# Paired 64-row mask products, filler work for TensorE, an early GpSimd drain, a last tile in halves and loads on release, in an attention-and-experts kernel

## The chip, the cores and the metric

The kernel runs on one core of one Trainium2 chip. The metric is the device time of one execution in microseconds (us). Each run comes with a state: **slow** runs (over 1.5% above the fastest of the same kernel on that chip) are left out of the comparisons of times here, and only times taken in the same call, on the same chip, are compared with each other. Traces are also read across chips, and three traces are of slow runs; the text says where. That turned out to matter: six calls on at least five chips appear below (the first call's chip is not on record), and the mean of the fast runs of the kernel before is 217 to 229 us, depending on the chip. In the five calls of the experiments these means rest on only 2 or 3 of its 7 to 11 runs, so ratios to the kernel before are uncertain by some 0.01 to 0.03; differences between variants of one call rest on 2 to 6 runs each.

A **hole** below is idle time of TensorE between two products. "issue" in a line means that the engine waited for nothing that the profile shows, and the granted clock is the share of full speed that the profile records for TensorE.

## The reference, cut to what matters

```python
# q, k, v: (4, 8, 768, 64).  Attention in a window of +-15 tokens, plus 24 block summaries
k_sum = k.reshape(B, H, 24, 32, D).max(axis=3);  v_sum = v.reshape(B, H, 24, 32, D).mean(axis=3)
scores = concat(where(abs(i - j) < 16, q k^T / 8, -1e9), q k_sum^T / 8 + log(32))
x = softmax(scores) @ concat(v, v_sum)          # -> (3072 tokens, 512)
# top-1 mixture of 8 experts, with a bias on the gate that depends on the token's modality
logits = x @ w_gate + modality_bias[modality_id];  e = argmax(logits)
out[t] = softmax(logits)[t, e] * relu(x[t] @ w1[e]) @ w2[e]      # w1: 512x1024, w2: 1024x512
```

With this draw all 3072 tokens go to two experts, 1564 to expert 3 and 1508 to expert 5. In tiles of 256 tokens that makes eleven full tiles, one of 228 and one of 28, and the one that comes last, the thirteenth, is that of 28.

## The kernel before

Sixteen **pairs** (a batch and two heads) go through the attention one after the other. For each, TensorE transposes k, v and q, forms scores in two halves, ScalarE takes the exponential into `pT`, and TensorE multiplies it with the values. From pair 10 on, expert work is put between the attention's steps in **units**, quarter tiles of the first layer or halves of the second. GpSimd issues the input and weight loads, scatters the finished rows into a sorted buffer `xs` with indirect DMAs, and stores each expert tile's result (`ot`) to `out` with indirect DMAs.

The parts that the change touches (cut):

```python
NMASK = 10
NV, NK = 8, 3                                   # input buffers: eight pairs deep
...
# keys(): two zero columns beside the transposed keys, one 128-wide product per tensor
nc.tensor.matmul(pb.bitcast(FP32)[:, 0:C8 * P8 // 2 + 2:C8 * P8 // 2 + 1],
                 ident[0:P8], identp[0:P8, 0:2], skip_group_check=True)
...
# scores(): the mask is added on TensorE for pairs 0 to 9, multiplied in on VectorE after that
if n < NMASK:
    for h in range(2):
        nc.tensor.matmul(pss[h], ident, bterm[:, 6 * half:6 * half + 6, :],
                         start=True, stop=False, skip_group_check=True)
for tl in range(6):
    for h in range(2):
        nc.tensor.matmul(pss[h][:, tl, :], kv[rr, 0, t, :], qT[...], start=n >= NMASK, stop=True, ...)
nc.scalar.activation(pT..., two, AF.Exp, scale=SCALE)
if n >= NMASK:
    nc.vector.tensor_tensor(pT[0:WK], pT[0:WK], bmask[...], op=ALU.mult)
...
UNITS = {10: "000111", 11: "111011", 12: "111011", 13: "111011", 14: "111011", 15: "101110"}
ENLIST = {9: 0, 11: 1, 15: 2}                   # after which pair a batch's tiles are listed
WAT = {2: "w0", 4: "w1", 6: "w2", 7: "w3", 8: "w4", 9: "w5", 10: "w6 w7"}   # weights in halves
def issue(n, i):
    if i < 3:
        if n + 4 < np_:
            load(n + 4, (i,))                   # inputs four pairs ahead
...
# the end: the thirteenth tile runs whole, all 256 rows
with ExitStack() as ifs:
    for j in range(NSURE, FIN):
        ifs.enter_context(tc.If(nt > j))
        ...
        drain(pending.popleft())
```

The softmax here doesn't subtract the row's maximum and nothing guards it: scores larger than these inputs give would overflow.

Of the kernel before, what the change touches and what calls it, by code (L numbers as in the profile page):

```python
# [18 lines left out]
TAKE = [2, 4, 2]  # L19
# [4 lines left out]
def kernel(  # L24
# [48 lines left out]
    NMASK = 10  # L73
    NV, NK = 8, 3
# [6 lines left out]
    def load(n, which=(0, 1, 2)):  # L81
        b, cc = pairs[n]
        for i in which:
            name, src = (("kn", k), ("vn", v), ("qn", q))[i]
            dst = work.tile([P8, 2, C8, D], FP16, tag=name, bufs=NV, name=name)
            nc.gpsimd.dma_start(
                dst.rearrange("p h c d -> p h (c d)"),
                src[b, 2 * cc:2 * cc + 2].rearrange("h (p c) d -> p h (c d)", c=C8),
            )
            loaded.setdefault(n, []).append(dst)  # L90
# [10 lines left out]
    identp = const.tile([128, 130], FP16, name="identp")  # L101
    ident = identp[:, 2:130]
    nc.vector.memset(identp[:, 0:2], 0.0)
    nc.vector.tensor_scalar(ident, cidx, pidx, None, op0=ALU.is_equal)

    def borders(i):
        kv, vb = kvs[i], vbs[i]
        nc.vector.memset(kv[:, :, :, KR:128], 0.0)
        nc.vector.memset(vb[0:WK, :, :, D:D + 1], 1.0)
        nc.vector.memset(vb[WK:KR, :, :, D:D + 1], 32.0)  # L110

    borders(0)
# [7 lines left out]
    band = const.tile([128, 2, 64], FP32, name="band")  # L120
    nc.vector.tensor_scalar(band[:, 0, :], cidx[:, 0:64], pidx, 0.0, op0=ALU.subtract, op1=ALU.is_lt)
    nc.vector.tensor_scalar(band[:, 1, :], cidx[:, 0:64], pidx, -32.0, op0=ALU.subtract, op1=ALU.is_gt)
    bmask = const.tile([128, NT, 64], FP16, name="bmask")
    nc.vector.tensor_tensor(bmask, band[:, 0:1, :].to_broadcast([128, NT, 64]),
                            band[:, 1:2, :].to_broadcast([128, NT, 64]), op=ALU.mult)
    edge = const.tile([128, 2], FP32, name="edge")
    nc.vector.tensor_scalar(edge[:, 0:1], pidx, 16.0, None, op0=ALU.is_ge)
    nc.vector.tensor_scalar(edge[:, 1:2], pidx, 80.0, None, op0=ALU.is_lt)
    nc.vector.tensor_scalar_mul(bmask[:, 0, :], bmask[:, 0, :], edge[:, 0:1])
    nc.vector.tensor_scalar_mul(bmask[:, NT - 1, :], bmask[:, NT - 1, :], edge[:, 1:2])  # L130
# [8 lines left out]

    bterm = const.tile([128, NT, 64], FP16, name="bterm")  # L140
    nc.vector.tensor_scalar(bterm, bmask, -1.0, 30000.0, op0=ALU.add, op1=ALU.mult)
    nc.vector.memset(bterm[WK:128], 0.0)

# [76 lines left out]
    def load_weights(u, e, which=(0, 1), part=None, **kw):  # L220
        for i in which:
            src, dst = ((moe_w1, w1b[u]), (moe_w2, w2b[u]))[i]
            src = src[ds(e, 1)].rearrange("a (c p) f -> p (a c) f", p=128)
            if part is not None:
                n = dst.shape[1] // 2
                src, dst = src[:, ts(part, n)], dst[:, ts(part, n)]
            nc.gpsimd.dma_start(dst, src, **kw)  # L227
# [4 lines left out]
    def keys(n):  # L232

        kv, vs = kvs[n % NK], None
        for i in range(2):
            src = loaded[n][i]
            pb = bank([128, 1024], FP16, "pk")
            for c in range(C8):
                for h in range(2):
                    nc.tensor.transpose(pb[64 * h:64 * h + 64, 2 + P8 * c:2 + P8 * c + P8], src[:, h, c, :],  # L240
                                        ident[0:P8, 0:P8])

            nc.tensor.matmul(pb.bitcast(FP32)[:, 0:C8 * P8 // 2 + 2:C8 * P8 // 2 + 1],  # L243
                             ident[0:P8], identp[0:P8, 0:2], skip_group_check=True)
            if i and n < NSUM:
                vs = pb[:, C8 * P8 + 4:C8 * P8 + 4 + 2 * NB].bitcast(FP32)
                for c in range(C8):
                    for h in range(2):
                        nc.tensor.matmul(vs[64 * h:64 * h + 64, :], src[:, h, c, :], ind[0:P8],
                                         start=(c == 0), stop=(c == C8 - 1), skip_group_check=True)  # L250
            nc.scalar.copy(  # L251
                kv[:, i, :, 0:WK].rearrange("p t (s c) -> p t s c", c=C8),
                bass.AP(pb.tensor, pb.offset, [pb.ap[0], [8, NT], [1, 12], [P8, C8]]))
        st[n] = dict(kv=kv, vb=vbs[n % NK], vs=vs)

    def summaries(n):
        kv = st[n]["kv"]
        ks = work.tile([128, 2, NT, 2], FP16, tag="ks", name="ks")
        nc.vector.reduce_max(ks[:, 0], kv[:, 0, :, 16:80].rearrange("p t (g s) -> p t g s", g=2), axis=AX.X)  # L259
        vs = st[n]["vs"]  # L260
        if vs is not None:
            nc.vector.tensor_copy(ks[:, 1].rearrange("p t g -> p (t g)"), vs)
        with nc.allow_low_precision(reason="summed in fp32, kept as v is"):
            vs is not None or nc.vector.reduce_sum(ks[:, 1], kv[:, 1, :, 16:80].rearrange("p t (g s) -> p t g s", g=2), axis=AX.X)  # L264
        nc.gpsimd.tensor_copy(kv[:, :, :, WK:KR],  # L265
                              ks.rearrange("p a t g -> p a (t g)")[:, :, None, :].to_broadcast([128, 2, NT, NB]))
# [11 lines left out]
    def blocks(n):  # L278

        kv, vb = st[n]["kv"], st[n]["vb"]  # L280
        for half in range(2):
            pv = bank([128, 6, 128], FP16, "pv")
            for tl in range(6):
                nc.tensor.transpose(pv[:, tl, :], kv[:, 1, 6 * half + tl, :], ident)  # L284
            (nc.vector.tensor_copy if half or n < NMASK and n % 4 else nc.scalar.copy)(  # L285
                vb[0:KR, 6 * half:6 * half + 6, :, 0:D],
                pv[0:KR].rearrange("p t (h d) -> p t h d", h=2))

    def scores(n, half):
# [4 lines left out]
        if n < NMASK:  # L294
            for h in range(2):
                nc.tensor.matmul(pss[h], ident, bterm[:, 6 * half:6 * half + 6, :],
                                 start=True, stop=False, skip_group_check=True)
        for tl in range(6):
            t = 6 * half + tl
            for h in range(2):  # L300
# [3 lines left out]
                                 start=n >= NMASK, stop=True, skip_group_check=True)  # L304
        pT = work.tile([128, 2, 6, 64], FP16, tag="pT", bufs=3, name="pT")
        nc.scalar.activation(pT.rearrange("p h t s -> p h (t s)"), two, AF.Exp, scale=SCALE)  # L306
        if n >= NMASK:
            nc.vector.tensor_tensor(
                pT[0:WK], pT[0:WK],
                bmask[0:WK, None, 6 * half:6 * half + 6, :].to_broadcast([WK, 2, 6, 64]), op=ALU.mult)  # L310
# [219 lines left out]
    def turn(i):  # L530
# [8 lines left out]
        (nc.scalar.copy if ended[0] >= sum(TAKE) - 4 else nc.vector.tensor_copy)(xg, px.rearrange("p c a s -> p c (a s)"))  # L539
# [38 lines left out]



    UNITS = {10: "000111", 11: "111011", 12: "111011", 13: "111011", 14: "111011", 15: "101110"}
    ENLIST = {9: 0, 11: 1, 15: 2}
# [64 lines left out]
    WAT = {2: "w0", 4: "w1", 6: "w2", 7: "w3", 8: "w4", 9: "w5", 10: "w6 w7"}  # L647

    def issue(n, i):
        if i < 3:  # L650
            if n + 4 < np_:
                load(n + 4, (i,))
            return
        for what in WAT.get(n, "").split():
            p = int(what[1:])
            if p % 4 == 0:
                gv[p // 4] = nc.gpsimd.value_load(guess[0:1, p // 4:p // 4 + 1], min_val=0, max_val=E - 1)
            load_weights(p // 4, gv[p // 4], which=(p // 2 % 2,), part=p % 2)
            if p == 3:
                guessed[0] = 1  # L660
            if p == 7:
                guessed[0] = NTILE + NWB
                ahead()
# [4 lines left out]
    load(3)  # L668
    borders(1)
    queries(0)  # L670
    side.append(early_constants())
    side.append(later_constants())
    for n in range(np_):
# [5 lines left out]
        issue(n, 0)  # L679
# [3 lines left out]
        issue(n, 1)  # L683
        tick(1 if n < 10 else 2)
        scatter()
        pump(u[1])
        if n == 0:
            keys(1)
            summaries(1)
            borders(2)  # L690
        if n + 1 < np_:
            queries(n + 1)
        if n:
            values(n - 1, 1)
# [5 lines left out]
        issue(n, 2)  # L700
        tick(1 if n < 10 else 2)
        scatter()
        pump(u[3])
        if n + 2 < np_:
            keys(n + 2)
        tick(1 if n < 10 else 2)
        pump(u[4])
        values(n, 0)
        issue(n, 3)
# [3 lines left out]
        if n + 2 < np_:  # L713
            summaries(n + 2)
        tick(1 if n < 10 else 2)
# [27 lines left out]
    while todo or len(pending) > 1:  # L743
        if ended[0] == i0 + NSURE - 2:
            nt = nc.values_load(r["li"][0:1, NSURE + 1, 0:1], min_val=NSURE, max_val=FIN)
        while unit():
            pass
    with ExitStack() as ifs:  # L748
        for j in range(NSURE, FIN):
            ifs.enter_context(tc.If(nt > j))  # L750
            if j == NSURE + 1:
                drain(take("more", r["cf"], FIN - NSURE - 1, i0 + j, KM))
            if j > NSURE:
                rows(lists["more"], j - NSURE - 1, i0 + j)
                weights(lists["more"], j - NSURE - 1, i0 + j)
                pending.append(expert_tile(i0 + j))
            drain(pending.popleft())
# [28 lines left out]
```

## Time and profile before

| | us |
|---|---|
| median of 3 runs | 229.16 (228.28 to 229.37) |
| span of the profiled execution | 226.3 |
| pair 1's to pair 10's first exponential | 53.80 |
| pair 10's first exponential to pair 11's | 14.15 |
| pairs 11 to 14 | 45.15 |
| end of the last store to the end | 9.4 |

The stages are cut at the start of a pair's first exponential. The view of busy times by stretch gives them; the columns are the stretch, its length, the busy time of TensorE's products, its weight loads, VectorE, ScalarE and GpSimd (instruction counts in brackets), the granted clock, the DMA engines' share and GB/s. For the kernel before:

```profile
19.14:72.94 53.80, 47.96 (x1257) 37.63 (x1252) 40.23 (x127) 41.27 (x51) 33.55 (x48) 0.92 1.00 161
72.94:87.09 14.15, 9.96 (x155) 8.14 (x154) 7.64 (x28) 6.45 (x9) 5.84 (x10) 0.58 0.96 181
87.09:132.24 45.15, 41.97 (x647) 29.18 (x645) 29.02 (x83) 29.63 (x45) 20.08 (x30) 0.97 0.53 126
```

In the first stretch TensorE works for 48 of 54 us and the DMA engines are full (share 1.00); in pair 10 the clock has fallen to 0.58.

### The profile page before, as it was taken

The numbers are of one execution on the slowest core, as the hardware profiler recorded it, in microseconds if no ns is written. First come the engines' busy times: TensorE is split into PE (matmuls) and PEld (weight loads), VectorE is DVE, ScalarE is ACT, GpSimd is POOL, SyncE is SP. The second block draws the span as 40 slices with busy tenths as digits, with TensorE's granted clock in tenths as the row PEclk, the third lists the DMA queues.
The fourth block names the chain that finished last, engine by engine and source line by source line (L and its number), as shares of the span: only waits on it lengthen the run. The fifth ranks groups of instructions, "written<-read, shape, count | busy, mean of one in ns | idle before, by whom it ended". The sixth has DMA issues, their size and how long they took to land. (4 is left out here: it accounts for less than half of the span.)

```text
span 226.3 us, 7116 instructions
## 1 busy us (share of the span) xinstructions
PE 189.3 (84%) x2948; PEld 136.1 (60%) x2948; DVE 104.5 (46%) x338; ACT 133.7 (59%) x180; POOL 111.3 (49%) x166
## 2 busy tenths in 40 slices
PE   0699998799895569999999599899976999999900
PEld 0487786587775458585767366675652766776500
DVE  6349975666994728784667182639200000000000
ACT  2589899458886428686675254455532667656410
POOL 8556545446895336680406507047673355462220
PEclk9999999859997559999999979999998899999975
DMA  4999999939999978998201303422333123321100
GB/s 74 178 185 151 130 185 171 190 53 147 225 163 206 226 159 133 206 157 256 104 3 72 122 1 118 125 89 80 122 106 138 51 91 120 112 82 54 53 19 0
DMA packets 20092, 27.47 MB, mean 121 GB/s; under 512 B 2876, under 2 KB 16468, under 8 KB 20052
## 3 DMA queue, kind: packets, MB, share of 16 engines
q0 software_dynamic: 17424, 24.40, 53.5%
q1 hardware_dynamic: 2628, 2.54, 3.9%
q8 instruction: 25, 0.41, 0.8%
q14 instruction: 15, 0.12, 0.2%
HBM read 85.46 MB, written 10.44 MB: 424 GB/s over the span
## 5 line engine op out<-in xcount | busy, mean ns | idle before, releaser
L556 PE MATMUL ph<-xg,w1b 128*128 128x256 f16 x416 | 51.7, 277 | 3.5 <-issue 1.7
L568 PE MATMUL pmo<-w2b,hT 128*128 128x512 f16 x208 | 49.8, 386 | 2.7 <-ACT hT L558 2.5
L556 PEld LDWEIGHTS <-w1b 128*128 128x128 f16 x416 | 39.7, 99 | 11.3 <-issue 3.0
L558 ACT ACTIVATE hT<-ph 128x512 f16<-128x512 f32 x52 | 31.0, 598 | 26.2 <-PE ph L556 18.4
L574 POOL DMA_INDIRECT out_dram<-ot,at x26 | 26.2, 1007 | 37.4 <-ACT ot L572 33.2
L251 ACT COPY kv<-pk 128x1152 f16<-128x1152 f16 x32 | 34.8, 1125 | 13.7 <-PE pk L243 10.7
L568 PEld LDWEIGHTS <-hT 128*128 128x128 f16 x208 | 19.5, 99 | 24.3 <-ACT hT L558 3.8
L572 ACT ACTIVATE ot<-pmo,xr 128x512 f32<-128x512 f32 x26 | 17.9, 690 | 24.7 <-PE pmo L568 16.5
L365 POOL DMA_INDIRECT xs<-xb,posi x24 | 25.8, 1074 | 13.1 <-issue 6.8
L306 ACT ACTIVATE pT<-pss 128x768 f16<-128x768 f32 x32 | 26.1, 816 | 7.2 <-PE pss L302 7.2
L265 POOL COPY kv<-ks 128x576 f16<-128x576 f16 x16 | 10.9, 683 | 39.2 <-DVE ks L264 15.8
L542 DVE SCALAR_TENSOR_TENSOR at<-gm,xr 128x2 uint32<-128x2 f32 x13 | 2.3, 182 | 40.9 <-DMA xr<-xs,gi 36.9
L332 DVE TENSOR_TENSOR xb<-po,rec 128x384 f16<-128x384 f32 x32 | 17.8, 556 | 1.0
L325 DVE RECIPROCAL rec<-po 128x6 f32<-128x6 f32 x32 | 6.1, 190 | 25.8 <-PE po L322 18.2
L275 ACT COPY qT<-pq 128x768 f16<-128x768 f16 x16 | 12.9, 809 | 7.8 <-PE pq L273 5.1
L259 DVE TENSOR_REDUCE ks<-kv 128x24 f16<-128x768 f16 x16 | 15.1, 944 | 3.0 <-ACT kv L251 3.0
L302 PEld LDWEIGHTS <-kv 64*128 64x128 f16 x384 | 8.3, 99 | 12.8 <-issue 11.8
L322 PE MATMUL po<-vb,pT 120*64 120x65 f16 x384 | 13.2, 203 | 3.2 <-issue 3.0
L284 PE MATMUL pv<-identp,kv 128*128 128x128 f16 x192 | 15.4, 236 | 0.0
L302 PE MATMUL pss<-qT,kv 64*128 64x64 f16 x384 | 12.5, 199 | 2.4 <-issue 2.2
L285 DVE COPY vb<-pv 120x768 f16<-120x768 f16 x23 | 12.2, 552 | 4.7 <-PE pv L284 4.5
L240 PE MATMUL pk<-identp,kn 96*64 96x96 f16 x256 | 9.3, 220 | 5.2 <-DMA kn<-in_k_dram 5.2
(130 smaller groups left out, 273.2 us busy)
## 6 DMA issues: line engine op xcount, KB each, us to landing
w1b<-in_moe_w_dram POOLq DMA_DIRECT2D x13, 1024.0 KB
w2b<-in_moe_w_dram POOLq DMA_DIRECT2D x13, 1024.0 KB
kn<-in_k_dram POOLq DMA_DIRECT2D x16, 192.0 KB
vn<-in_v_dram POOLq DMA_DIRECT2D x16, 192.0 KB
qn<-in_q_dram POOLq DMA_DIRECT2D x16, 192.0 KB
xr<-xs SPq DMA_DIRECT2D x8, 272.0 KB, 3.9
w1b<-in_moe_w_dram POOLq DMA_DIRECT2D x4, 512.0 KB
w2b<-in_moe_w_dram POOLq DMA_DIRECT2D x4, 512.0 KB
```

The lines of the kernel that those rows point to most:

```text
L251: nc.scalar.copy(kv[:, i, :, 0:WK].rearrange("p t (s c) -> p t s c", c=C8), bass.AP(pb.tensor, pb.offset, [pb.ap[0], [8, NT], [1, 12], [P8 ...
L259: nc.vector.reduce_max(ks[:, 0], kv[:, 0, :, 16:80].rearrange("p t (g s) -> p t g s", g=2), axis=AX.X)
L284: nc.tensor.transpose(pv[:, tl, :], kv[:, 1, 6 * half + tl, :], ident)
L302: nc.tensor.matmul(pss[h][:, tl, :], kv[rr, 0, t, :], qT[rr, ts(t, 8), :].rearrange("p s c -> p (s c)"), start=n >= NMASK, stop=True, skip ...
L306: nc.scalar.activation(pT.rearrange("p h t s -> p h (t s)"), two, AF.Exp, scale=SCALE)
L332: nc.vector.tensor_tensor(xo, po[:, :, :, 0:D], rec.unsqueeze(3).to_broadcast([128, 2, 3, D]), op=ALU.mult)
L365: apart("xs", nc.gpsimd.indirect_dma_start(out=xs[:, :], out_offset=bass.IndirectOffsetOnAxis(ap=posi[:, j:j + 1], axis=0), in_=xb[:, c, : ...
L556: nc.tensor.matmul(ph[:, f, :], w1[:, c, ts(2 * f2 + f, 128)], xg[:, c, :], start=(c == 0), stop=(c == NCD - 1))
L558: nc.scalar.activation(hT[:, 2 * f2:2 * f2 + 2, :], ph, AF.Relu)
L568: nc.tensor.matmul(po, hT[:, f, ts(s2, 128)], w2[:, f, :], start=(f == 0), stop=(f == NF - 1))
L572: nc.scalar.activation(ot, po, AF.Copy, scale=gt)
L574: apart("out", nc.gpsimd.indirect_dma_start(out=out[:, :], out_offset=bass.IndirectOffsetOnAxis(ap=at[:, s2:s2 + 1], axis=0), in_=ot[:], i ...
```

## The change

Its intent is to take work and waits off TensorE: two 64-row mask products side by side (the traces show starts 3 ns apart, and 173 ns apart for the two before) in place of one 128-row product each; filler products before the data arrive, so that the clock is full when they do (its records begin, with full speed, at 5.34 us instead of 13.17); expert work a pair later, so that it doesn't wait for its rows; loads issued when a buffer is released, weights in quarters; the thirteenth tile in halves of 128 tokens, the second skipped if empty; and GpSimd's DMA queue drained some tiles before the end. Smaller parts aren't shown: in pairs 10 to 15 VectorE takes over most of ScalarE's copies of v, ScalarE copies the first expert tile's rows, and GpSimd clears a strip of the keys and values in each pair. The core of it (cut):

```diff
-    NMASK = 10
-    NV, NK = 8, 3
+    NV, NK = 3, 3
...
+    busy(9)                       # 9 products of 512 columns on zeros, 3 more within pair 0's keys
...
-            nc.tensor.matmul(pb.bitcast(FP32)[:, 0:C8 * P8 // 2 + 2:C8 * P8 // 2 + 1],
-                             ident[0:P8], identp[0:P8, 0:2], skip_group_check=True)
+            for h in range(2):
+                nc.tensor.matmul(pb[64 * h:64 * h + 64].bitcast(FP32)[:, 0:C8 * P8 // 2 + 2:C8 * P8 // 2 + 1],
+                                 src[:, h, C8 - 1, :], warm[0:P8, 0:2], skip_group_check=True)
...
-        if n < NMASK:
-            for h in range(2):
-                nc.tensor.matmul(pss[h], ident, bterm[:, 6 * half:6 * half + 6, :], ...)
+        for h in range(2):
+            rr = slice(64 * h, 64 * h + 64)
+            nc.tensor.matmul(pss[h], bterm[rr, :], ident[rr, None, rr].to_broadcast([64, 6, 64]), ...)
...
-        if n >= NMASK:
-            nc.vector.tensor_tensor(pT[0:WK], pT[0:WK], bmask[...], op=ALU.mult)
...
-    UNITS = {10: "000111", 11: "111011", 12: "111011", 13: "111011", 14: "111011", 15: "101110"}
-    ENLIST = {9: 0, 11: 1, 15: 2}
+    UNITS = {11: "111111", 12: "111111", 13: "111111", 14: "111111", 15: "101110"}
+    ENLIST = {9: 0, 12: 1, 15: 2}
...
-    WAT = {2: "w0", 4: "w1", 6: "w2", 7: "w3", 8: "w4", 9: "w5", 10: "w6 w7"}
+    WAT = {1: 1, 2: 1, 3: 1, 4: 2, 5: 1, 6: 2, 7: 2, 8: 2, 9: 2, 10: 2}      # quarters
+    def more(n, which):           # called where a buffer's last reader has been issued
+        if n + NV < np_:
+            load(n + NV, which)
...
-        scatter()
+        early = n - 1 not in ENLIST
+        scatter(early)            # and a second scatter(early) later in the pair
...
         if ended[0] == last - 2:
             nt = nc.values_load(...)
+            more_than = left(r, NSURE)
+            nc.gpsimd.drain()
...
-            drain(pending.popleft())
+            expert_half(i, 0)
+            with tc.If(more_than > 128):
+                expert_half(i, 1)
```

## The prediction

> **What bounds the kernel now.** I read the sliced page first (where is TensorE not full, where is its clock low), then the TensorE timeline around every hole, then the pair periods, and last the end. The page's slices (5.66 us each):
>
> ```profile
> PE   0699998799895569999999599899976999999900
> ACT  2589899458886428686675254455532667656410
> PEclk9999999859997559999999979999998899999975
> DMA  4999999939999978998201303422333123321100
> ```
>
> TensorE is full nearly everywhere, so it is the bound, except in the first slice, around slices 12 to 14, at slice 22 and in the last two. The clock digit dips exactly beside those holes. The timeline of TensorE shows what one hole costs (start us, us; the bracket is the idle time before the group):
>
> ```profile
> 43.39 0.30 PE L302 MATMUL pss<-qT,kv 64*128 64x64 f16 x9 [1.45 <-issue]
> 46.13 0.82 PE L296 MATMUL pss<-bterm,identp 128*128 128x384 f16 x2
> ...
> 55.99 0.50 PE L296 MATMUL pss<-bterm,identp 128*128 128x384 f16 x2
> 56.42 0.35 PE L302 MATMUL pss<-qT,kv 64*128 64x64 f16 x12
> ...
> 71.97 0.43 PE L322 MATMUL po<-vb,pT 120*64 120x65 f16 x8 [2.31 <-issue]
> ...
> 80.98 1.03 PE L537 MATMUL px<-identp,xr 128*128 128x128 f16 x8 [4.18 <-DMA xr<-xs]
> ```
>
> After the 1.45 us hole the same two mask products take 0.82 instead of 0.50: the clock records have half speed from 43.6 to 50.4 us, and again from 70.9 to 84.5. The first two holes fall within a run of like products ("issue"), each within 1 us of a 16 KB packet on TensorE's instruction queue: I take them for instruction fetches held up while the DMA row above is at 9. The third is the first expert tile's rows.
>
> The chain of waits reaches back only to 203.85 us and is GpSimd's output stores, so I take the end from the timeline:
>
> ```profile
> 207.83 3.66 PE L556 MATMUL ph<-xg,w1b 128*128 128x256 f16 x32
> 211.32 3.62 PE L568 MATMUL pmo<-w2b,hT 128*128 128x512 f16 x16
> 215.03 0.69 ACT L572 ACTIVATE ot<-pmo,xr 128x512 f32<-128x512 f32 x1 [1.04 <-PE pmo L568]
> 215.99 0.98 POOL L574 DMA_INDIRECT out_dram<-ot,at  x1 [0.75 <-ACT ot L572]
> ```
>
> The thirteenth expert tile takes 7.1 us of TensorE, and 9.4 us lie between its last store (216.97) and the end of the span (226.34). The trace's own instruction records, which count as idle in the views, put into this 9.4 us an INC_SWDGE_SEM of 1.36 us and, after all data have landed (last packet 217.98), a GpSimd DRAIN of 4.81 us. The two drains right after it take 0.10 and 0.05, and the one at the kernel's start 0.18.
>
> [...] the 128-row mask pair needs 0.43 from start to start[...]; and the zero-column product (N of 2) inside the 64-column transposes costs 0.10. [...]
>
> **The change part by part.**
>
> *Head.* k lands at 5.23 us, v at 7.06, q at 9.36 (waits of TensorE), and the clock is half until 12.9: 0.85 for 16 transposes that later take 0.53. Nine 512-column fillers at about 0.43 cold (twice the 0.216 from start to start of the second layer's products) are 3.8 us, so they end near 5 us, just when k lands. Warm, v's transposes and sums (1.55) shrink to 0.95, but q's landing then sets the first scores, 0.15 earlier than 10.89 at most; scores and block transposes up to 12.9 gain another 1.0, of which ScalarE, continuous from 13.7, keeps half. **-0.7.**
>
> *Masks, pairs 0 to 9.* Two half-array products at once: one stream of 0.16 plus some 0.04, against 0.43. That is 0.46 a pair of TensorE. The zero columns become two small products [...]: I guess 0.05 saved on each of two a pair, 0.1. Undisturbed pairs take 4.9 us (28.68 to 33.58) with TensorE busy throughout and ScalarE 4.36 of it (5.0 in every fourth), so ScalarE stops the gain: 4.9 to 4.5, nine pairs, **-3.6.**
>
> *Masks, pairs 10 to 15.* There TensorE is the bound with expert work beside it (10.5 to 11 us a pair), and now it masks too: 12 halves x 0.2 = +2.4, zero columns -0.5. The twelve DVE products of 0.55 that go were beside TensorE's work and free nothing. **+1.9.**
>
> *Experts a pair later.* Units start in pair 11, 24 in pairs 11 to 14 where 20 were. TensorE's sum is unchanged; what goes is that it stands 4.18 us for rows that landed 8.0 us after pair 10's first exponential. The new place is one pair of about 5 us later, so up to 1 us may stay. The half clock from 81 to 84.5 goes too (two groups of 0.85 for 0.53, one of 1.59 for 1.03: 1.4). **-4.5.**
>
> *Loads on release, weights in quarters.* The bytes are the same; 512 KB pieces no longer stand in a lump ahead of fetches and rows. The two fetch holes cost 1.45 + about 2.6 (6.8 us at half clock) and 2.31 + about 1.8. A fetch still comes every 5 us or so into a full DMA, so I count half of 8.1: **-4.0.**
>
> *Last tile in halves.* I counted the draw: experts 3 and 5 get 1564 and 1508 tokens, so the thirteenth tile has 28, and its second half is skipped. First layer: 32 products of 128 columns at 0.055 (the block transposes' spacing, 12 in 0.83) = 1.8; then ScalarE's second Relu at about 2.7; then the last 4 of 8 products, 0.9: 3.65 instead of 7.1. **-3.4.**
>
> *Drain.* If its 4.8 us is work heaped up by some 140 GpSimd DMAs, the early one takes it away from the end and leaves perhaps 0.5: -4.3, which I give 7 chances in 10, so -3.0. But it stands on GpSimd's queue at about 195.3 us, before the weight issue of tile 11 (196.31) and the gather of tile 12, which landed at 201.28 and is used by the transposes at 203.93: slack 2.65, so 4.8 of drain could hold TensorE up by about 2.1 us. I count +1.5. **-1.5.**
>
> Sum: -0.7 -3.6 +1.9 -4.5 -4.0 -3.4 -1.5 = -15.8. From 229.16 that is 213.4; the holes at 124 to 129 us (3 us, "issue") and at 166.9 and 173.5 (1.34 and 2.12) I leave as they are. I say **213 us.**
>
> **Rivals.** (1) *ScalarE becomes the bound in the first ten pairs.* For: 4.4 to 5.0 us busy in pairs of 4.9. Against: it still has 0.2 to 0.5 us holes there. Taken fully, the -3.6 shrinks to about -1.5, total 215. (2) *The stalls only move.* For: DMA stays at 9 until 110 us, and fetches and rows share it. Then the -4.0 and half of the -4.5 are lost: 219. (3) *The drain costs the same wherever it stands*, because it is no backlog: no gain and a stall, 215 to 217. Against: the short drains after the long one. (4) *All holes close* and ScalarE keeps up: the other half of the 8.1, 1 us more of the rows and 2 of drain, 206. A transfer bound is unlikely: pair 10 needs about 7 MB of inputs and 3 MB of weights by then, some 50 us at the 190 GB/s of the busy slices, and it starts at 73 now.
>
> **Range and chances.** Fetch luck is worth 4 either way, drain 3, masks 2, rows 2; combined about 5.7 as a root of squares, and 1.2 of that on each side for 8 in 10: 206 to 220. Faster by over 2% means below 224.6, which needs nearly three quarters of the sum to fail: 0.95. The halves alone give 1.5%, so slower is 0.01.
>
> **What the profile after would show.** Head: transposes of the first pair at 0.53 and the clock full from about 5 us. Masks: 64-row mask products on 64 instructions, with pair starts 0.2 to 0.25 apart from the scores, and undisturbed pairs of about 4.5. Rows: no wait over 1 us for xr before the first expert tile. Fetch: no "issue" hole over 1 us, no half clock between 40 and 85 us. End: the last tile under 4 us, and a final drain under 1 us with one of 4 to 5 us some 20 us earlier. Wrong would be: "issue" holes as long as before, pairs still 4.9 with ScalarE full, or a last drain as long as before.

## The result, and the profile after

| | before | after |
|---|---|---|
| median of 4 runs, us | 229.26 (228.28 to 232.66) | 221.62 (219.7 to 223.22) |
| span of the profiled execution | 226.3 | 219.2 |

The ratio is 0.965, interval 0.956 to 0.975. Ratios here are the mean time of one kernel's fast runs over that of the other's of the same rounds, so not quite the ratio of the medians. Faster was right, 213 us was not: 221.62 is above the 206 to 220 that were expected.

The slices of the kernel after (40 of 5.5 us; TensorE, its clock, the DMA engines):

```profile
PE   7679778798779669978999739999785999998860
...
PEclk9997999959979999999999966999999999999997
DMA  5999999998999999737200323203243222220220
```

The first slice has work (0.7 of it), and the clock records begin with full speed at 5.34 us, as hoped. But TensorE then stands at 6 to 9 through the next 14 slices, where before most were 9, and there is a dip to 3 in slice 24, with the clock at 6 in slices 24 and 25. The same stretches as before:

```profile
17.30:71.56 54.26, 45.33 (x1318) 39.34 (x1316) 42.29 (x129) 40.91 (x50) 37.51 (x63) 0.89 1.05 170
71.56:76.88 5.32, 3.38 (x113) 2.81 (x111) 5.01 (x24) 4.32 (x7) 2.95 (x8) 1.00 1.12 213
76.88:135.81 58.93, 50.04 (x709) 33.49 (x710) 27.76 (x83) 31.68 (x47) 25.38 (x40) 0.94 0.52 129
```

TensorE's work in pairs 1 to 9 fell from 47.96 to 45.33 us, yet the stage takes 54.26 instead of 53.80. Its clock is 0.89: the clock records show half speed from 42.9 to 49.7 us and from 63.4 to 66.8, right after holes of 1.50 and 1.12 us, where the prediction had expected none. A third stretch of it, 15.6 to 19.0, comes after a hole of 1.41; one of 1.44 that ended at 26.5 us was not followed by any, and in the kernel before one of 1.45, ending at 43.4, was. These stretches last 3.4 or 6.8 us. Where the 7.1 us of the two spans come from:

| stage (first exponentials as marks) | before | after | difference | predicted |
|---|---|---|---|---|
| start to pair 1 | 19.14 | 17.30 | -1.8 | -0.7 |
| pairs 1 to 9 | 53.80 | 54.26 | +0.5 | -7.6 |
| pairs 10 to 14 (after has 24 units here, before 23) | 59.30 | 64.25 | +4.9 | -2.6 |
| pair 15 to the end of the last store | 84.73 | 78.3 | -6.5 | -3.4 and +1.5 |
| from there to the end | 9.4 | 5.1 | -4.2 | -3.0 |

So two rows fail, by about 8 us each, and the other three give more than they were to (pair 15 has one unit less to do than before). The first two rows vary from profile to profile: in ten profiles below whose kernels are the same up to pair 10 (one of them a slow run), the start takes 17.3 to 18.7 us and pairs 1 to 9 take 51.1 to 55.7; the kernel before has 53.8 and, on another chip, 57.1 there. So the +0.5 is uncertain by 2 or 3 us, but a gain of 7.6 is not there. The timeline of TensorE (start, length, work; in brackets the idle time before it and what ended it) around one pair of the failing stage, kernel after:

```profile
29.66 0.34 PE L307 MATMUL pss<-ident,bterm 64*128 64x384 f16 x2
29.83 0.34 PE L313 MATMUL pss<-qT,kv 64*128 64x64 f16 x12
30.10 0.40 PE L246 MATMUL pk<-ident,kn 96*64 96x96 f16 x9
31.61 0.36 PE L246 MATMUL pk<-ident,kn 96*64 96x96 f16 x7 [1.11 <-issue]
...
36.44 0.20 PE L313 MATMUL pss<-qT,kv 64*128 64x64 f16 x1 [0.97 <-issue]
```

The mask pair does what was promised: the scores start 0.17 us after it, where they had started 0.43 after. But then TensorE stands in the middle of a run of like products, waiting for nothing that the profile shows.

Counting products from the start places these holes. They stand at product 222, 350, 478, 606, 734 and 862, 128 apart each time, and TensorE's instruction queue moves 16 KB packets, one for each. A 16 KB packet is thus 128 weight loads and 128 products. In each case a packet starts 0.8 to 1.9 us before the hole begins, and TensorE goes on 2.2 to 2.8 us after the packet's start. The packet itself starts 1.2 to 3.9 us after TensorE has passed the boundary before, in this stage; in the two runs of the fifth call, wherever the DMA engines stood idle at that moment, it started after 0.6 us or less. So a block of 128 products takes about 3.5 to 6.5 us to come beside busy DMA engines and, as an estimate from these figures, up to about 3.5 us on idle ones. The kernel before has the same holes at products 734, 862, 1245 and 1501 (0.72, 1.45, 0.64, 2.31 us); after has them at most boundaries of the first stage, 0.3 to 1.5 us each. The profile labels some of them by a wait for VectorE or ScalarE that happened to end last; the position and the packet tell what they are.

The rows for the first expert tile came nearly as hoped, 1.86 us late instead of 4.18:

```profile
78.08 0.62 PE L544 MATMUL px<-ident,xr 128*128 128x128 f16 x8 [1.86 <-DMA xr<-xs]
```

The dip in slice 24 is of another kind. TensorE and GpSimd, kernel after, in pair 14:

```profile
122.56 2.46 PE L563 MATMUL ph<-xg,w1b 128*128 128x256 f16 x16
126.04 0.24 PE L329 MATMUL po<-vb,pT 120*64 120x65 f16 x2 [1.02 <-issue]
127.48 0.19 PE L329 MATMUL po<-vb,pT 120*64 120x65 f16 x1 [1.21 <-issue]
...
130.34 0.42 PE L329 MATMUL po<-vb,pT 120*64 120x65 f16 x7 [1.16 <-issue]
```

```profile
124.27 0.99 POOL L581 DMA_INDIRECT out_dram<-ot,at  x1 [0.30 <-issue]
...
125.56 0.98 POOL L372 DMA_INDIRECT xs<-xb,posi  x1 [0.28 <-issue]
126.84 0.98 POOL L372 DMA_INDIRECT xs<-xb,posi  x1 [0.30 <-DVE tk L508]
```

This is a second kind of hole, no longer 128 products apart: TensorE gets one product at a time, every 0.5 to 1.4 us, for 4.4 us in all, exactly while GpSimd works off a queue of indirect DMAs back to back, one each 1.29 us. ScalarE's instructions are late in the same way: it stands for 3.52 and 3.83 us before two of them, and its exponential starts at 130.50, though the scores for it ended at 122.64. VectorE's are not: twelve start from 124.12 to 126.60 with no idle time that the view shows between them. Over the whole trace such holes sum to 10.8 us (96 to 99, 108, 125 to 130, 154, 164 and 168 us), and half the clock from 128.2 to 135 costs another 3.4. In the kernel before they are fewer: about 2 us at 125 to 128 and 0.5 at 141, and the waits that end at 166.9 and 173.5 (1.34 and 2.12) fall into such runs too, 5.9 us in all, with half clock from 129.2 to 132.6 and from 173.6 to 177.0, another 3.4.

The end, kernel after:

```profile
208.36 1.95 PE L595 MATMUL ph<-xg,w1b 128*128 128x128 f16 x32
...
210.15 1.89 PE L600 MATMUL pmo<-w2b,hT 128*128 128x512 f16 x8
...
212.12 0.69 ACT L602 ACTIVATE ot<-pmo,xr 128x512 f32<-128x512 f32 x1 [1.18 <-PEq L801]
213.08 0.98 POOL L603 DMA_INDIRECT out_dram<-ot,at  x1 [2.54 <-ACTq L801]
```

The last tile takes TensorE 3.68 us (208.36 to 212.04) instead of 7.1. In the trace's instruction records the early drain takes 4.41 us at 193.41 and the last one 0.64 instead of 4.81. TensorE's two waits behind the early one, for the weights at 199.6 and the gathered rows at 204.5, are 0.61 and 0.71. Not predicted: after the last store GpSimd is done with it at 214.1 and stands until TensorE's last conditional branch, 4.36 us long from 212.23, has been taken. A 16 KB instruction packet comes in at 213.25.

### The profile page after: what moved, and what is told of

It reads as the page before. It is cut to its first block, busy times and chain, and to the rows that moved or that the text cites. A ratio compares the mean times of both kernels' runs of the same rounds, so it can differ in the third digit from the quotient of the medians.

```text
span 219.2 us, 7344 instructions
## 1 busy us (share of the span) xinstructions
PE 181.5 (83%) x3008; PEld 130.9 (60%) x3008; DVE 99.8 (46%) x335; ACT 129.4 (59%) x174; POOL 116.5 (53%) x189
## 5 line engine op out<-in xcount | busy, mean ns | idle before, releaser
L563 PE MATMUL ph<-xg,w1b 128*128 128x256 f16 x384 | 46.9, 273 | 4.2 <-issue 2.6
L575 PE MATMUL pmo<-w2b,hT 128*128 128x512 f16 x192 | 46.8, 390 | 2.7 <-issue 2.4
L563 PEld LDWEIGHTS <-w1b 128*128 128x128 f16 x384 | 35.9, 98 | 12.3 <-issue 5.8
L565 ACT ACTIVATE hT<-ph 128x512 f16<-128x512 f32 x48 | 28.5, 599 | 23.0 <-PE ph L563 17.9
L581 POOL DMA_INDIRECT out_dram<-ot,at x24 | 23.8, 992 | 31.2 <-ACT ot L579 19.6
L579 ACT ACTIVATE ot<-pmo,xr 128x512 f32<-128x512 f32 x24 | 16.4, 688 | 22.8 <-PE pmo L575 9.5
L296 DVE COPY vb<-pv 120x768 f16<-120x768 f16 x28 | 14.6, 553 | 6.9 <-PE pv L295 6.8
L295 PE MATMUL pv<-ident,kv 128*128 128x128 f16 x192 | 15.5, 237 | 0.3 <-issue 0.3
L329 PEld LDWEIGHTS <-pT 120*64 120x64 f16 x384 | 10.4, 118 | 8.0 <-issue 7.6
L276 POOL COPY kv<-ks 128x576 f16<-128x576 f16 x16 | 10.8, 678 | 7.9 <-DVE ks L275 4.1
L295 PEld LDWEIGHTS <-kv 128*128 128x128 f16 x192 | 13.1, 107 | 1.7 <-issue 0.6
```

Source lines behind the costliest of these rows:

```text
L295: nc.tensor.transpose(pv[:, tl, :], kv[:, 1, 6 * half + tl, :], ident)
L329: nc.tensor.matmul(po[64 * (tl % 2):64 * (tl % 2) + 64, h, tl // 2, :], pT[0:KR, h, tl, :], vb[0:KR, 6 * half + tl, h, :])
L563: nc.tensor.matmul(ph[:, f, :], w1[:, c, ts(2 * f2 + f, 128)], xg[:, c, :], start=(c == 0), stop=(c == NCD - 1))
L565: nc.scalar.activation(hT[:, 2 * f2:2 * f2 + 2, :], ph, AF.Relu)
L575: nc.tensor.matmul(po, hT[:, f, ts(s2, 128)], w2[:, f, :], start=(f == 0), stop=(f == NF - 1))
L579: nc.scalar.activation(ot, po, AF.Copy, scale=gt)
```

## The experiments

Two theories came out of the comparison. **Full DMA**: in pairs 1 to 9 the instruction blocks come late because the DMA engines are full, and work saved between two blocks is lost in the wait for the next. **Indirect runs**: from pair 11 on, GpSimd's indirect DMAs in a row keep the other engines' instructions from coming. The rivals are the ordinary ones: ScalarE bounds the first pairs; the masks, the loads or the number of instructions did harm themselves; the drain and the expert order cost what they save. Expectations are quoted as they were put on record before each run.

### First call (chip 3): one part undone at a time

Four variants of the changed kernel, without the changed kernel beside them. The kernel before had 216.75 here in its fast runs (2 of 7).

**No sums on TensorE** (fewer instructions: VectorE sums v instead):

```diff
-    NSUM = 12
+    NSUM = 0
```

> The changed kernel with the sums of v taken by VectorE (as it does in its last four pairs) instead of by 16 small matmuls a pair: some 122 matmuls a pair instead of 138. Theory F (TensorE's program comes in blocks of 128 matmuls[...]; in the loaded first 75 us a block takes 5 to 6 us to come, so pairs 1 to 9 can't go faster than their blocks): pairs 1 to 9 fall from 54.3 us to 49 or 50, ratio to before 0.945 to 0.95. Rival C (the chain through ScalarE, VectorE and GpSimd sets these pairs): VectorE has 0.8 us more a pair, so pairs stay or grow, ratio 0.965 to 0.98.

**The old loads** (eight buffers, four pairs ahead, weights in halves):

```diff
-    NV, NK = 3, 3
+    NV, NK = 8, 3
-    WAT = {1: 1, 2: 1, ...}  # quarters, loads on release
+    WAT = {2: "w0", 4: "w1", ...}  # halves; load(n + 4, (i,)) in the pair's steps as before
```

> The changed kernel with the loads of the kernel before (eight buffers, four pairs ahead, weights in halves from pair 2 on). Theory L (the new order of loads puts more into the DMA queues before 25 us, so that instruction blocks wait longer): the holes in TensorE at block boundaries before 45 us, 7.2 us in the changed kernel, fall to 3 or less as before, and the ratio to before from 0.965 to about 0.95. Theory S (the DMA engines are full in either order, and the holes come of TensorE needing its blocks sooner): holes stay at 6 to 8 us, ratio 0.96 to 0.975.

**The old 128-row mask** in pairs 0 to 9:

```diff
-            nc.tensor.matmul(pss[h], bterm[rr, :], ident[rr, None, rr].to_broadcast([64, 6, 64]), ...)
+            if n < 10:
+                nc.tensor.matmul(pss[h], ident, btall[:, None, :].to_broadcast([128, 6, 64]), ...)
+            else:
+                nc.tensor.matmul(pss[h], bterm[rr, :], ident[rr, None, rr].to_broadcast([64, 6, 64]), ...)
```

> The changed kernel with 128-row masks in pairs 0 to 9 (same number of matmuls, 0.26 us more of TensorE a half). Theory F (instruction blocks bound these pairs): the holes shrink by what the products grow, pairs 1 to 9 within 1.5 us of 54.3, ratio 0.96 to 0.972. The prediction's theory (TensorE's work bounds them): 18 halves x 0.26 = 4.7 us longer, ratio 0.985.

**No early drain** (the line with `nc.gpsimd.drain()` taken out):

> The changed kernel without the early GpSimd drain. Theory B (a drain works off what GpSimd's DMAs have heaped up since the last one): the last drain goes back from 0.64 to 4.5 to 4.8 us, and the 1.6 us of TensorE waits at 199 to 204.5 us go, so 2.5 us longer in all, ratio 0.976. Rival: a drain costs what it costs wherever it stands and the end got shorter for another reason: last drain stays under 1 us and the time falls by 1.5 us, ratio 0.958.

| chip 3, fast runs | mean us | ratio to before | pair 10's first exponential |
|---|---|---|---|
| no sums on TensorE | 205.3 (4) | 0.945 | 71.1 |
| old loads | 203.9 (1) | none | 71.1 (trace of a slow run) |
| old mask | 207.1 (3) | 0.961 | 70.8 |
| no early drain | 209.5 (4) | 0.967 | 72.8 |

All four reached pair 10 at 71 to 73 us: neither fewer instructions, nor the old loads, nor the slower mask moved the first stage by more than it varies anyway (pairs 1 to 9 took 51.0 to 54.2 us in the four). There was no control on this chip, so its times say nothing on what a part is worth. The lesson that I hadn't planned for was in the level: all four ran at 204 to 210 us, and in none of their traces did TensorE stand behind indirect DMAs. Chips seem to differ in that (each was seen in one call, so chip and call can't be told apart), and so the next calls carried the changed kernel as a control.

### Second call (chip 2): controls, the old expert order, the last tile whole

> The kernel before, unchanged, for a profile on the chip of this call, since the last call's chip ran it in 220 us instead of 229. If that difference is of the chip's supply of instructions, the holes of TensorE while GpSimd issues runs of indirect DMAs (2.2 us at 124 to 128 us, and 2 to 3 us at 160 to 175 us on the first chip) are missing or small; if it is of the clock or of DMA, they are as before and something else is shorter.

> The changed kernel, unchanged, on this call's chip. If the failure of the prediction lies in what a chip adds (holes during runs of indirect DMAs: 7.5 us in pairs 12 to 15 of the changed kernel, with 3.4 us of half clock, against 2.2 us and 1.7 before), then on a chip without them the gain is larger: 13 to 15 us, ratio 0.935 to 0.945. If it lies in the blocks of instructions of the first ten pairs alone, the ratio stays at 0.96 to 0.97.

**Expert work in pair 10 as before:**

```diff
-    UNITS = {11: "111111", 12: "111111", 13: "111111", 14: "111111", 15: "101110"}
-    ENLIST = {9: 0, 12: 1, 15: 2}
+    UNITS = {10: "000111", 11: "111011", 12: "111011", 13: "111011", 14: "111011", 15: "101110"}
+    ENLIST = {9: 0, 11: 1, 15: 2}
-        scatter(early)
+        scatter()          # and no second one
```

> The changed kernel with the experts started in pair 10 and the scatter slots of the kernel before. The prediction's theory: TensorE waits 3 to 4.5 us for the first rows again, 2 to 4 us longer than the changed kernel. Rival: the wait only moved (1.9 us of it was left in the changed kernel, and one pair more of expert work lies behind the loop's chain), so within 1.5 us of the changed kernel.

**The thirteenth tile whole:**

```diff
-            expert_half(i, 0)
-            with tc.If(more_than > 128):
-                expert_half(i, 1)
+            drain(keep.pop())
```

> The changed kernel with the thirteenth expert tile whole, as before. The prediction's step: the tile takes 7.1 us instead of 3.7 of TensorE, one more store, so 3.4 us longer than the changed kernel in the end section. Rival (a new wait after the second branch ate part: 3.6 us pass between the GpSimd's store and the end of the wait at the branch, against 1.6 before): only 1.5 to 2 us longer.

The changed kernel took 222.9 us (3 fast runs), ratio 0.972 to the 229.2 of the kernel before; its one profiled run, c_before, took 231.99. That trace answers its expectation: the holes behind indirect DMAs are there as on the first chip, about 7 us between 127 and 178 us. With the old expert order 227.1 (2 fast runs), so that part is worth 4.3, give or take 4. The traces of the control and of the old order fell in the slow state, so I read them only against each other: the wait for the first tile's rows is back, at 8.3 us, and pairs 11 to 14 took 46.2 us for 20 units, against 61.6 for 24 in the control, with holes behind indirect DMAs: in pair 14's run of them TensorE loses 4.5 us in the control and 1.5 with the old order. The later order thus gains at pair 10 and gives part of it back there. With the last tile whole 226.0 (3 fast runs): the halves are worth 3.1, again give or take 3; in the traces the stretch from pair 15 to the end of the last store is 82.3 against 78.8 us (a slow run), and the tile takes 7.1 us of TensorE again.

### Third call (chip 13): the two causes

> The changed kernel again, as the control of this call's chip. On chip 2 it was 0.972 of before; on a chip like 3, whose kernels showed no holes during runs of indirect DMAs, theory K (those holes, 5 to 8 us on chip 2, are what keeps the changed kernel from its gain) expects 206 to 207 us beside 217 to 220, ratio 0.94.

**Weights later**, to free the DMA engines in the first stage:

```diff
-    WAT = {1: 1, 2: 1, 3: 1, 4: 2, 5: 1, 6: 2, 7: 2, 8: 2, 9: 2, 10: 2}
+    WAT = {3: 1, 5: 1, 7: 1, 8: 1, 9: 2, 10: 4, 11: 6}
...                                # and ahead() is called after the eighth quarter too
```

> The changed kernel with the speculative weights issued later: 6 of 16 quarters by pair 9, 10 in pairs 10 and 11, instead of 14 by pair 9. Theory D (the DMA engines, not TensorE or any chain, bound the first ten pairs, so that instruction blocks wait behind loads): some 2.1 MB at 180 GB/s less, so pair 10's first exponential comes at 65 to 68 us instead of 71 to 72, and the holes at block boundaries halve; the end by 0 to 4 us earlier, as the weights may be waited for in pairs 11 and 12. Theory F alone (a block's latency is what it is): pair 10 stays at 71 or 72.

**Shorter runs of indirect DMAs** in pair 14:

```diff
         scatter(early)
+        if n == 14:
+            early = 0
...
-        if u[3]:
+        if u[3] and n != 14:
             scatter(2)
```

> The changed kernel with three of the third batch's six scatters put off from pair 14 to pair 15, so that GpSimd's run of indirect DMAs in pair 14 is shorter. Theory K: on a chip that shows the holes (4.4 us at 125 to 130 and half clock to 135), pair 14 shortens from 19 to 15 or 16 us and the whole by 2 to 4 us. Rival: the holes have another cause and stay, time within 1 us. On a chip without them: no difference.

**Output stored without indirect DMAs** (wrong on purpose: SyncE stores plain blocks, to the wrong rows):

```diff
-            apart("out", nc.gpsimd.indirect_dma_start(out=out[:, :], out_offset=..., in_=ot[:], ...))
+            nc.sync.dma_start(out[256 * (i % 12) + 128 * s2:256 * (i % 12) + 128 * s2 + 128], ot)
```

> The changed kernel with the output stored by plain DMAs from SyncE's queue, to the wrong rows (wrong on purpose), so that GpSimd issues 24 indirect DMAs fewer and its runs break up. Theory K: on a chip that shows holes during runs, all 'issue' holes after 95 us but those at 155 to 168 (scatters and gathers of the last batch) go, 5 to 8 us shorter. Rival (SyncE's DMAs take the same toll): holes stay. On a chip without them: within 2 us of the changed kernel.

| chip 13, fast runs | mean us | pair 10's first exponential | pairs 11 to 14 |
|---|---|---|---|
| kernel after | 222.4 (3) | 69.9 | 61.5 |
| weights later | 232.6 (3) | 68.5 | |
| shorter runs | 217.4 (2) | 69.0 | 57.2 |
| no indirect output stores | 210.4 (3) | 70.0 | 55.6 |

Without the 25 indirect stores 12 us are gone, so **the indirect runs are the cause** of the second kind of hole, not a neighbour of it. The traces say the same: the holes of 0.3 us and more in such runs sum to about 13 us in this call's control and to 2.9 without the stores. (Those stores also no longer queue behind the scatters and the drain, so a part of the 12 may be theirs.) What is left stands beside six scatters in a row; pair 14 without the stores:

```profile
122.18 0.29 PE L313 MATMUL pss<-qT,kv 64*128 64x64 f16 x4 [0.52 <-issue]
...
127.33 0.54 PE L329 MATMUL po<-vb,pT 120*64 120x65 f16 x12
```

Splitting the longest run in two is worth 5.1, though from two fast runs, and the holes in pair 14 fall from 4.5 to 2.0 us. The weights issued later were a miss: the first stage gained only 1.4 us, less than it varies, and then TensorE stood for weights, 4.88 and 3.11 us. Either the DMA wasn't the reason, or taking some weights away left it full.

### Fourth call (chip 4): masks, drain and a combined version, with a control

> The changed kernel itself, as the control on this chip: 0.955 to 0.975 of the kernel before. If this chip is one where a run of indirect DMAs does not hold the sequencers up (as the first one of the variants was), it lands nearer 0.95.

**Shorter runs, and the drain one tile later:**

```diff
+        if n == 14:
+            early = 0                          # and no scatter(2) in pair 14
...
-            nc.gpsimd.drain()                  # at ended[0] == last - 2
+        if ended[0] == last - 1:
+            nc.gpsimd.drain()
```

> The scatters of pair 14 in smaller lots, and the GpSimd drain one expert tile later. Theory (long runs of indirect DMAs starve TensorE's sequencer, and the drain only has to stand ahead of the end): faster than the changed kernel by 1 to 5 us, 0.94 to 0.96 of the kernel before, with no wait of TensorE over 0.3 us for w1b or xr after 195 us, and the last drain still under 1.5 us. Rival (the drain's place costs the same anywhere, and the runs of indirect DMAs do no harm): the same as the changed kernel within 0.5%.

The old mask and the missing drain again, the same edits as on chip 3:

> The 128-row mask product in pairs 0 to 9 again, with the changed kernel beside it on the same chip. Prediction as recorded (0.46 us a pair of TensorE's time counts in nine pairs): 3.6 us slower than the changed kernel. Rival (in these pairs the arrival of TensorE's instruction blocks through a full DMA sets the pace): within 1 us of it, with tenth pair's first exponential less than 1 us later.

> The early GpSimd drain left out, with the changed kernel beside it on the same chip. As predicted (4.3 us come back at the end, 1.5 us of stall are saved): 2.8 us slower. If the drain that ends the program is followed in any case by other work of about the same length (TensorE's and ScalarE's own last instructions): within 1 us of the changed kernel, with the last drain at 4 to 5 us.

| chip 4, fast runs | mean us | ratio to before | against the kernel after |
|---|---|---|---|
| kernel before | 219.3 (3) | | |
| kernel after | 205.2 (5) | 0.936 (0.923 to 0.948) | |
| shorter runs, later drain | 205.4 (6) | 0.938 | +0.3 |
| old mask | 206.6 (6) | 0.941 | +1.4 |
| no early drain | 208.5 (5) | 0.954 | +3.4 |

Here **the same change gains 14.2 us**. The kernel after, on this chip, TensorE and GpSimd in pair 14, and then its pairs 1 to 9 and 11 to 14:

```profile
118.71 1.92 PE L563 MATMUL ph<-xg,w1b 128*128 128x256 f16 x16
120.56 0.38 PE L329 MATMUL po<-vb,pT 120*64 120x65 f16 x12
```

```profile
118.07 0.98 POOL L581 DMA_INDIRECT out_dram<-ot,at  x1 [0.30 <-ACT qT L286]
119.35 0.99 POOL L372 DMA_INDIRECT xs<-xb,posi  x1 [0.30 <-issue]
```

```profile
18.61:71.34 52.73, 43.89 (x1281) 38.48 (x1274) 41.25 (x129) 40.55 (x50) 38.08 (x64) 0.84 1.06 174
...
77.36:123.89 46.53, 44.91 (x704) 31.66 (x700) 27.65 (x83) 31.39 (x46) 23.44 (x38) 1.00 0.55 136
```

It is the same instruction stream in the same place: sixteen products of the first layer in 1.92 us instead of 2.46, twelve of the values in 0.38 instead of 4.7, and all the while a run of indirect DMAs at the same 1.29 us. This chip lets TensorE's instructions through. Pairs 11 to 14 take 46.53 us instead of the 58.93 on the first chip. Pairs 1 to 9 don't differ: 52.73 and 54.26, DMA share 1.06 and 1.05.

The combined version brought nothing here, where no holes were there to remove; its later drain moved the two waits of 0.61 and 0.87 us into one of 1.48 for the thirteenth tile's weights. The old mask costs 1.4, between the 3.6 of the prediction and the rival's less than 1, and hardly more than its own uncertainty (about 1.4); in its trace pair 10's first exponential comes 2.2 us later (73.5 against 71.3), of which 0.9 in pairs 1 to 9, again within what these stages vary. The drain is worth 3.4 (about 1.6 either way): the last DRAIN falls from 4.73 to 0.64 us and two semaphore instructions ahead of it from 1.33 to 0.33 each, and from the last store's start to the end of the span it is 6.0 instead of 11.6 us; the two waits of TensorE, 1.5 in all, go off that.

### Fifth call (chip 1): the input traffic taken away

The question left open by the third call: is the full DMA the reason for the late instruction blocks? And what are the masks worth once it is gone?

```diff
         for i in which:
+            if n >= 3:
+                loaded.setdefault(n, {})[i] = kept[n % 3, i]      # no load: wrong on purpose
+                continue
```

> Wrong on purpose: pairs 3 to 15 reuse the q, k and v of pairs 0 to 2 already loaded, so the input transfers of 13 of 16 pairs fall away; all instructions of TensorE, ScalarE and VectorE and the expert tiles stay. Theory (in pairs 1 to 9 TensorE's 16 KB instruction blocks come late because the DMA engines are full): the holes at block boundaries shrink below 0.5 us, undisturbed pairs of 4.2 to 4.5 run in a row, and pair 10's first exponential comes at 55 to 60 us instead of 68 to 72; the experts may then wait for weights instead. Rival (ScalarE's or GpSimd's own work, or the blocks themselves, set the pace, whatever the DMA does): 66 to 72 us as before.

The second run of this call has that edit and the old 128-row mask in pairs 0 to 9.

> The same reuse of loaded inputs (wrong on purpose), with the 128-row mask product of the kernel before in pairs 0 to 9. If the masks' 0.46 us a pair is real and only the late blocks hide it, pair 10's first exponential comes 3 to 4 us later than in the run with 64-row masks. Rival (ScalarE bounds the pairs, so that TensorE's saving is worth nothing even then): less than 1 us later.

Fast runs: 197.8 us (3) with 64-row masks and 199.0 (3) with 128-row masks; the kernel before had 218.3 here. Pair 1's to pair 10's first exponential, without the input loads (64-row masks), and then pairs 2 and 4 alone:

```profile
18.02:62.34 44.32, 41.28 (x1319) 36.54 (x1318) 41.42 (x129) 39.94 (x49) 20.49 (x36) 0.97 0.52 92
```

```profile
24.03:28.25 4.22, 4.13 (x143) 3.67 (x140) 4.15 (x12) 4.22 (x7) 1.37 (x3) 1.00 0.24 31
...
32.47:37.25 4.78, 4.30 (x149) 3.95 (x150) 3.58 (x11) 4.78 (x7) 1.29 (x3) 1.00 0.38 59
```

Pairs 2, 3 and 4 with the 128-row masks:

```profile
23.41:28.02 4.61, 4.61 (x144) 3.69 (x142) 4.39 (x12) 4.36 (x7) 1.36 (x3) 1.00 0.31 49
28.02:32.51 4.49, 4.49 (x142) 3.56 (x140) 3.82 (x10) 4.32 (x6) 1.31 (x3) 1.00 0.47 73
32.51:37.29 4.78, 4.76 (x144) 3.79 (x141) 3.58 (x11) 4.78 (x7) 1.28 (x3) 1.00 0.38 59
```

With the DMA share halved, to 0.52, the stage takes 44.32 us with the same instructions of TensorE, where it took 51.1 to 55.7; between 10 and 44 us TensorE has no hole over 0.3 us at all. **The full DMA is the reason**, and it costs some 7 to 11 us. Against the first chip's trace it is 9.9: 5.9 of idle time and 4.0 of products that last longer (45.3 us of work instead of 41.3) at a mean granted clock of 0.89 instead of 0.97. The edit also takes the issuing of these loads off GpSimd, a rival that it doesn't exclude by itself. But in these two runs four packets started 0.3 to 0.6 us after the boundary while GpSimd was issuing a weight load and the DMA engines still stood idle, so issuing alone doesn't hold a block up. Pair 10 came at 62.3, not at the 55 to 60 that the theory had said, because of what the other two fences show: now ScalarE is busy for 4.22 of 4.22 us. With the old masks TensorE is full instead, at 4.61 and 4.49, and every fourth pair, where ScalarE copies once more, is 4.78 either way. The masks are worth 0.95 us over the nine pairs (44.32 against 45.27, one profile each) and 1.2 in the fast runs' means, which these runs' scatter of 2.8 us doesn't resolve. My 3 to 4 us were wrong; pair 10 came 0.2 us later with the old masks (62.56), after a start that was 0.7 earlier, so the rival, ScalarE, had it nearly right.

## Why the prediction was right or wrong

**Head (-0.7): held**, and a bit more: 1.15 us at pair 0's first exponential, 1.8 at pair 1's (0.4 to 1.8 over the ten profiles). Pair 0's transposes take 0.53 to 0.55 us instead of 0.85, and the clock records show full speed from 5.34 us on instead of 13.17, so the filler work did bring the full clock.

**Masks, pairs 0 to 9 (-3.6): the mechanism held, the size failed.** The step "ScalarE stops the gain: 4.9 to 4.5, nine pairs" took a pair of 4.9 us as the undisturbed one. Undisturbed, with the old masks, a pair is 4.5 to 4.6, and every fourth 4.8. With the new ones it is 4.2, ScalarE's own time, and 4.8. That is 1.0 us in nine pairs, as the fifth call shows on a DMA half as busy; the 1.4 of chip 4, on a full one, is not clear of noise. It is rival (1), taken further than I took it. That two 64-row products run side by side is shown by the trace after: the pair's starts lie 3 ns apart, with 0.17 us from the pair to the scores. In the trace before, the two heads' 64-row score products start 3 ns apart too (30.408 and 30.411 us).

**Loads on release, quarters (-4.0): failed.** The step "512 KB pieces no longer stand in a lump ahead of fetches" is where it broke. The old trace showed four holes at block boundaries and I counted two. Beside busy DMA engines a block comes 3.5 to 6.5 us after the boundary before. With slower pairs most blocks seem just to have made it. With faster ones nearly all show, at 0.3 to 1.5 us each, and half clock followed three of them (1.41, 1.50 and 1.12 us), though not one of 1.44. The order of the loads is not the point (the old loads reached pair 10 at 71.1 us and kept 7.6 us of holes before 45 us); the traffic is, as the fifth call shows. The prediction had also set a bound by transfers aside, from 10 MB at 190 GB/s in some 50 us. By the views of stretches (154 GB/s up to pair 1, 170 from there) the kernel after had moved about 11.9 MB when pair 10 began, at 71.6 us: the transfers did set the pace, through the program and not through late inputs. Rival (2), "the stalls only move", was the right one, and at 219 it was the nearest to what came. (Two small slips of reading: the prediction counts slices from 0, and by the views the two stretches of half clock last from 43.9 to 50.7 and from 71.2 to 84.8 us, 0.3 later than it says.)

**Experts a pair later (-4.5): held as a net,** 4.3 on chip 2, give or take 4. The wait for rows shrank to 1.86, a bit more than the 1 us allowed.

**"The holes at 124 to 129 us ... I leave as they are": failed, and it was the largest miss on the first chip.** They were an effect that the change itself makes bigger: with 24 units in pairs 11 to 14, more output stores fall in with the scatters, and GpSimd's queue grows into longer runs (4.5 us of holes in pair 14 on chip 2, 1.5 with the old order). The whole trace of after has 10.8 us of such holes, plus 3.4 us of half clock. On a chip that lets instructions through there is no such loss: 14.2 us gained on chip 4. That this is near the 15.8 of my sum is luck: pairs 1 to 9, with 7.6 of the 15.8, take 52.7 us there too. I have no trace of the kernel before on such a chip, so how that 14.2 is spread over the stages stays open.

**Masks, pairs 10 to 15 (+1.9): not measured by itself.** TensorE is busy for 44.91 of 46.53 us in pairs 11 to 14 on chip 4, which fits TensorE as the bound there.

**Halves (-3.4): held,** 3.1, give or take 3, and 3.68 us of TensorE for the tile where 3.65 were expected. **Drain (-1.5): the mechanism held, the size was too small:** 3.4 on chip 4. In these runs the last drain was short when one had been made 16 to 27 us earlier (0.2 to 0.7 us, after 6 to 12 more DMAs), which fits the backlog that I gave 7 in 10. But a drain is not simply as long as the number of DMAs before it: 6.7 us after 100 of them without the input loads, 4.4 after 139. The stall was 1.3 to 1.5, less than the 2.1 worked out, and the semaphore instructions ahead of the last drain fell too. Part of it stays hidden behind TensorE's last branch (4.36 us in the kernel after).

Put together for the first chip: from -15.8, masks 2.6 and loads 4.0 go off, and the indirect runs cost about 5 more than before (10.8 and 3.4, against 5.9 of holes and waits and 3.4 of half clock there); drain and head give back 3. That makes about -7, and -7.1 was measured. Several of these terms are uncertain by 2 or 3 us, so the close agreement is partly luck, and the stage table above is the firmer account.

What makes one chip pass instructions during indirect DMAs and another not stays open; no run here varies it. So does the version to prefer: the one with shorter runs beat both kernels on chip 13 (217.4 against 222.4 and 226.7), and with the later drain it equals the changed kernel on chip 4. Shorter runs with the drain left where it was would be the choice; that was run on one chip only.

## What to carry to other kernels

A hole labelled "issue" is worth counting in instructions: here the holes recurred every 128 products, each with a 16 KB packet of TensorE's instruction queue, so the program itself arrived late; less DMA traffic helped (pairs 1 to 9 in 44.3 us instead of 51 to 56), and fewer instructions for TensorE did not (pair 10 at 71.1 us without the sums). Before shortening an engine's part, compare a pair's length with the busy time of the next engine (here 4.2 us of ScalarE), because that is where the gain ended. And check what a tighter schedule does to the queue of indirect DMAs, on more than one chip: the same change was worth 3.5% on one and 6.5% on another.
